# Gate products by tile, three experts set apart, a wider pace of side work, and TensorE given products from the start

## The chip, the cores and the metric

The kernel runs on one core of one Trainium2 chip. The metric is the device time of one execution in microseconds (us). The program works on five engines: TensorE (PE in the rows: matmuls and transposes into PSUM), VectorE (DVE), ScalarE (ACT), GpSimd (POOL) and SyncE (SP, which issues most DMAs). Each engine takes its instructions in the order in which the program wrote them, and waits for the others by semaphores.

## The reference

Three stages in float32. `x` is (4, 8, 512, 64), `state` is (4, 8, 32, 64).

```python
# 1. attention between x and a small state, both ways
a  = softmax(x @ state.T / 8);  xread = a @ state
a2 = softmax(state @ x.T / 8);  sread = a2 @ x
x1 = concat([xread, sread], axis=2)            # -> 2176 rows of 512
# 2. eight experts, every row through all of them, weighted by a Sinkhorn-balanced gate
P = exp(x1 @ w_gate - max)                     # (2176, 8)
for _ in range(8):
    P /= P.sum(1) + 1e-9;  P /= P.sum(0) + 1e-9;  P *= N / E
out = sum_e P[:, e] * (relu(x1 @ w1[e]) @ w2[e])
# 3. the same sizes again, but each row goes to its argmax expert alone
```

w1 is (8, 512, 1024) and w2 is (8, 1024, 512) in both expert stages.

## The kernel before

The 2176 rows are 17 tiles of 128 (`t`). Stage 2 runs in three passes over the rows: tiles 0 to 5, 6 to 11 and 12 to 16. A pass has 32 steps `s`: eight experts, and for each the hidden width in four quarters of 256. A step consists of two parts. `mm1(s)` makes the hidden quarter: seven products of halves of the operands (a scheme that needs seven where the plain one needs eight), each in three float32r matmuls for two halves of the contraction, since every operand is split into a high part and a low part (`XR` holds both for x, `HB` for the hidden values). `mm2(s, t)` multiplies the hidden quarter by w2 for one row tile and adds it to `acc`, weighted by `PG[:, t, e]`, the balanced gate. TensorE runs `mm1(s + 1)` before `mm2(s)`.

Ahead of pass 0 stands the attention for batches 0 and 1 (groups named `A0`, `A1`, `C0`, `C1` in the code, five pieces each: transposes of x (`psx`), scores (`pss`), softmax on VectorE and ScalarE, transposes (`psa`), the read (`pso`)). From its result `xst`, `xsums` and `xsplit` make the seven x operands of pass 0: four sums or differences, seven rounded copies on ScalarE (L390) and seven low parts (L392), of which three go to GpSimd.

All the rest of stage 1 and the gate is side work: it stands in a list named `queue`, and is handed out between the parts of the steps of pass 0. `pump(dt)` adds a nominal time `dt` to a credit (1.04 us for a product of `mm1`, 1.36 us for a tile of `mm2`) and takes one item from the list whenever the credit reaches `pace`. So a small `pace` puts the items close together. The list of before is: the gate products of tiles 0 to 3, 4 to 5 and 6 to 7, the attention of batches 2 and 3 (`window`), the state reads, the gate of tile 16, `close_reads` (which gives back the attention's memory and takes the buffer `raw2` there), and the Sinkhorn steps. The pace is 66 divided by the number of items until `close_reads`, and 2.4 after it.

The Sinkhorn loop is eight times `row` (five small VectorE operations, the last of which, L332, makes column sums) and `col` (a TensorE product `pscol` with a matrix of ones at L337, and four small VectorE operations). Pass 0 must have `PG` when it weights its first expert. Before, the experts 0 and 1 of pass 0 are summed without weight, expert 0 in `acc` and expert 1 in the memory of `xst`, and are weighted at expert 2 (L541, L542), that is in `mm2(8)`; the list is emptied before step 9.

The lines that the steps of the prediction touch: L137 (ScalarE issues the loads of the state), L390 and L392 (operands of pass 0), L376 to L379 (their sums), L432 (GpSimd, low part of the weight sums of the next step), L303 (gate products), L328 to L341 (Sinkhorn), L536 to L547 (what `mm2` does with its PSUM bank).

Of the kernel before, what the change touches and what calls it, by code (L numbers as in the profile page):

```python
# [21 lines left out]
def tile_state_attention_moe_moe2(  # L22
# [104 lines left out]

    def constants():
        make_identity(nc, ident)
        nc.vector.memset(ones, 1.0)  # L130

# [13 lines left out]
    def routing_constants():  # L145
        fl = dict(allow_small_or_imprecise_dtypes=True)
        nc.gpsimd.memset(onesb, 1.0)
        nc.gpsimd.memset(lowb, 1.0)
# [162 lines left out]
    def sinkhorn():  # L311
# [31 lines left out]

        steps += [s0, s1]
        for i in range(8):
            steps += [row, col(i)]
        return steps
# [33 lines left out]

    def xsplit(p, t, order=(0, 4, 3, 5, 1, 2, 6), pool=(3, 1, 6)):
        b11, b12, b21, b22, w = xquarters(p)
        of = [b11, b21, b22] + t

        def one(i):
            def f():
                hi = xop(i, 0, w).rearrange("p (k n) -> p k n", k=2)
                lo = xop(i, 1, w).rearrange("p (k n) -> p k n", k=2)
                nc.scalar.copy(hi, of[i])  # L390
                e = nc.gpsimd if i in pool else nc.vector
                e.tensor_tensor(out=lo, in0=of[i], in1=hi.bitcast(F32), op=ALU.subtract)  # L392
            return f
        return [one(i) for i in order]
# [58 lines left out]
    def mm1(s, between):  # L453
# [39 lines left out]
        between(3)  # L493
        prod(2, B_[1], start=False)
        tt(out=c22, in0=B_[5], in1=u3, op=ALU.add)
        relu(B_[1], 0, 0)
        relu(c22, 1, 1)
        between(4)
        new(3)
        rest(B_[1], 0, 0)  # L500
        tt(out=u4, in0=B_[3], in1=u4, op=ALU.add)  # L501
# [371 lines left out]
    with tc.manual_schedule():  # L873
        accf = acc.rearrange("p a c -> p (a c)")
        crit, lag = {}, {}
        for b in range(B):
            for g in range(G):
                crit[b, g], lag[b, g] = attention(b, g)
        load_x(0, 0)
        constants()  # L880
        load_state(0)
# [26 lines left out]
        A0[4]()  # L908
        A1[4]()
        C0[3]()  # L910
        C1[2]()
        C1[3]()
        C0[4]()
        C1[4]()
        sums, T0 = xsums(0, accf)
        parts = xsplit(0, T0)
        parts[0]()
# [29 lines left out]
        def window(b):  # L947
# [4 lines left out]
            def nx(g, f):  # L952
                def h():
# [7 lines left out]
                    c[1], n20, e[1], c[2], n21, e[2], c[3], nx(0, n30), e[3],  # L961
                    nx(1, n31), c[4], e[4], gate(range(4 * b, 4 * b + 4))]

        home = [None]

        def close_reads():
# [5 lines left out]
            smp[0] = rtp[0]  # L972
            pace[0] = 2.4
            raw2 = ctx.enter_context(tc.tile_pool(name="raw2", bufs=1, side="right", reuse_waits="tile")).tile(
# [52 lines left out]
        queue += window(2) + window(3)  # L1027
        (a0, a1, a2), (b0, b1, b2) = lag[2, 0], lag[2, 1]
        queue += [a0, b0, a1, b1, seq(a2, lambda: load_x(3, 0)), seq(b2, lambda: load_x(3, 1))]
        (a0, a1, a2), (b0, b1, b2) = lag[3, 0], lag[3, 1]  # L1030
        queue += [a0, b0, a1, b1, a2, b2, seq(gate(range(NT - 1, NT)), states_out)]
# [186 lines left out]
```

## Time and profile before

| | |
|---|---|
| median of 3 runs | 1878.95 us (1878.01 to 1881.89) |
| the profiled execution, its own time | 1879.49 us |
| its span in the trace | 1877.8 us |
| TensorE busy | 1804.5 us, 96% of the span |
| VectorE, ScalarE, GpSimd busy | 65%, 35%, 59% |
| granted TensorE clock, mean | 0.973 of full speed |
| the chain that ended last | TensorE 74%, VectorE 9%, issue 9%, DMA 5% |

TensorE is busy nearly all the time, so time can only be lost where it is idle or where it runs at half clock. In the page's forty slices its row falls below 9 tenths at the beginning, in the slices after 200 us, at the two changes of pass (about 660 and 1200 us) and in the last fifth; the granted clock is lowest in the first two slices. A matmul's busy time at half clock counts as busy, and the two must be read together.

### The profile page before, as it was taken

The numbers are of one execution on the slowest core, as the hardware profiler recorded it, in microseconds if no ns is written. First come the engines' busy times: TensorE is split into PE (matmuls) and PEld (weight loads), VectorE is DVE, ScalarE is ACT, GpSimd is POOL, SyncE is SP. The second block draws the span as 40 slices with busy tenths as digits, with TensorE's granted clock in tenths as the row PEclk, the third lists the DMA queues.
The fourth block names the chain that finished last, engine by engine and source line by source line (L and its number), as shares of the span: only waits on it lengthen the run. The fifth ranks groups of instructions, "written<-read, shape, count | busy, mean of one in ns | idle before, by whom it ended". The sixth has DMA issues, their size and how long they took to land.

```text
span 1877.8 us, 25502 instructions
## 1 busy us (share of the span) xinstructions
PE 1804.5 (96%) x9327; PEld 1607.7 (86%) x9327; DVE 1211.8 (65%) x2041; ACT 653.3 (35%) x1114; POOL 1099.3 (59%) x857
## 2 busy tenths in 40 slices
PE   7998899999999999999999999799999999899998
PEld 5997788999999889999999998689999899778886
DVE  5664769666666676666666666896666666745332
ACT  3432222333333333333333333333333343345333
POOL 2432456666776566666667765577787877412212
PEclk8799899999999999999999999899999999999999
DMA  4243112322222222222222222232222222245122
GB/s 113 74 107 96 51 45 68 102 68 68 68 68 68 90 80 71 70 71 96 68 68 68 68 67 84 67 129 81 80 79 79 90 79 68 76 137 199 62 81 89
DMA packets 126618, 154.65 MB, mean 82 GB/s; under 512 B 41424, under 2 KB 91600, under 8 KB 123920
## 3 DMA queue, kind: packets, MB, share of 16 engines
q1 hardware_dynamic: 121920, 142.41, 24.2%
q0 software_dynamic: 3280, 10.23, 1.7%
q8 instruction: 75, 1.23, 0.3%
q14 instruction: 63, 0.52, 0.1%
q10 hardware_dynamic: 1280, 0.26, 0.1%
HBM read 138.99 MB, written 14.42 MB: 82 GB/s over the span
## 4 chain that ended last, share of the span: by engine, by line
PE 74%; DVE 9%; issue 9%; DMA 5%; POOL 2%; ACT 1%; SPq 0%; POOLq 0%; DVEq 0%; ACTq 0%
PE py L527 12%; PE py L528 12%; PE py L529 12%; PE p L465 11%; PE p L467 11%; PE p L466 11%; DMA out_dram<-xst,si 4%; DMA out_dram<-y,si 1%; DVE HB L478 1%; PE psg L303 1%; PE psr L281 1%; PE pss L206 1%; PE pl L576 1%; DVE acc L547 1%; PE pso L243 1%
## 5 line engine op out<-in xcount | busy, mean ns | idle before, releaser
L443 POOL TENSOR_TENSOR wl<-rawb,wh 128x1024 fp32r<-128x1024 f32 x96 | 230.8, 2405 | 473.1 <-ACT wh L442 473.1
L465 PE MATMUL p<-XR 128*128 128x384 f32 (+1 forms) x1344 | 447.9, 333 | 4.2 <-ACT XR L390 2.8
L467 PE MATMUL p<-XR 128*128 128x384 f32 (+1 forms) x1344 | 444.1, 330 | 4.1 <-POOL XR L432 3.0
L466 PE MATMUL p<-XR 128*128 128x384 f32 (+1 forms) x1344 | 443.7, 330 | 0.9 <-DVE XR L392 0.9
L527 PE MATMUL py<-wh,HB 128*128 128x512 f32 x1088 | 431.6, 397 | 2.4 <-DVE acc L547 2.3
L528 PE MATMUL py<-wl,HB 128*128 128x512 f32 x1088 | 429.0, 394 | 0.0
L529 PE MATMUL py<-wh,HB 128*128 128x512 f32 x1088 | 428.6, 394 | 0.0
L547 DVE SCALAR_TENSOR_TENSOR acc<-py,PG,acc 128x512 f32<-128x512 f32 x485 | 338.9, 741 | 79.3 <-PE py L529 78.7
L432 POOL TENSOR_TENSOR XR<-sst,XR 128x1024 fp32r<-128x1024 f32 x96 | 255.0, 2656 | 50.8 <-ACT XR L426 50.8
L465 PEld LDWEIGHTS p<-XR 128*128 128x128 f32 x1344 | 256.8, 191 | 11.3 <-ACT XR L390 4.1
L467 PEld LDWEIGHTS p<-XR 128*128 128x128 f32 x1344 | 256.5, 191 | 5.4 <-POOL XR L432 3.8
L466 PEld LDWEIGHTS p<-XR 128*128 128x128 f32 x1344 | 256.7, 191 | 4.9 <-DVE XR L392 1.5
L478 DVE SCALAR_TENSOR_TENSOR HB<-u,HB 128x384 fp32r<-128x384 f32 (+1 forms) x192 | 169.3, 883 | 117.4 <-ACT HB L474 117.2
L529 PEld LDWEIGHTS py<-wh,HB 128*128 128x128 f32 x1088 | 206.7, 190 | 44.2
L527 PEld LDWEIGHTS py<-wh,HB 128*128 128x128 f32 x1088 | 206.8, 190 | 44.0 <-DVE acc L547 3.0
L528 PEld LDWEIGHTS py<-wl,HB 128*128 128x128 f32 x1088 | 206.6, 190 | 39.7
L483 ACT COPY u<-p 128x384 f32<-128x384 f32 (+1 forms) x96 | 44.3, 461 | 527.6 <-PE p L467 523.5
L428 POOL TENSOR_TENSOR XR<-rawb,XR 128x512 fp32r<-128x512 f32 x96 | 141.6, 1475 | 7.4 <-ACT XR L422 7.4
L426 ACT CAST XR<-sst 128x1024 fp32r<-128x1024 f32 x96 | 100.8, 1050 | 93.7 <-POOL sst L421 93.7
L474 ACT ACTIVATE HB<-u 128x384 fp32r<-128x384 f32 (+1 forms) x192 | 96.9, 505 | 80.0 <-DVE u L501 72.2
L486 DVE TENSOR_TENSOR u<-p,u 128x384 f32<-128x384 f32 (+1 forms) x96 | 51.3, 534 | 112.6 <-PE p L467 108.2
L474 ACT ACTIVATE HB<-p 128x384 fp32r<-128x384 f32 (+1 forms) x96 | 45.5, 474 | 190.4 <-PE p L467 190.4
(292 smaller groups left out, 2491.4 us busy)
## 6 DMA issues: line engine op xcount, KB each, us to landing
rawb<-in_moe_w_dram SPq DMA_DIRECT2D x192, 512.0 KB, 3.5
raw<-in_moe_w_dram SPq DMA_DIRECT2D x15, 1024.0 KB, 6.4
xb<-in_x_dram SPq DMA_DIRECT2D x60, 128.0 KB, 3.1
rawb<-in_moe_w_dram SPq DMA_DIRECT2D x5, 1024.0 KB, 5.1
x1d<-acc SPq DMA_DIRECT2D x16, 256.0 KB, 2.4
xtd<-xtm SPq DMA_DIRECT2D x4, 512.0 KB, 3.0
x1p<-acc SPq DMA_DIRECT2D x8, 256.0 KB, 2.6
xst<-xtd SPq DMA_DIRECT2D x1, 1536.0 KB, 8.3
```

The costliest lines, as they stand in the source:

```text
L428: nc.gpsimd.tensor_tensor(out=wop(s, 1, 0, 2).rearrange(r, k=KD), in0=raw[:, :, 0:P], in1=wop(s, 0, 0, 2).rearrange(r, k=KD).bitcast(F32), ...
L432: nc.gpsimd.tensor_tensor(out=wop(s, 1, 3, 4), in0=sst.rearrange("p a c -> p (a c)"), in1=wop(s, 0, 3, 4).bitcast(F32), op=ALU.subtract)
L443: nc.gpsimd.tensor_tensor(out=lo, in0=raw, in1=hi.bitcast(F32), op=ALU.subtract)
L465: nc.tensor.matmul(ps, wh, xh, start=start and k == 0, stop=False, skip_group_check=True)
L466: nc.tensor.matmul(ps, wh, xl, start=False, stop=False, skip_group_check=True)
L467: nc.tensor.matmul(ps, wl, xh, start=False, stop=stop and k == 1, skip_group_check=True)
L474: nc.scalar.activation(out=hh[:, f, half * h : (half + 1) * h], in_=c, func=AF.Relu)
L478: nc.vector.scalar_tensor_tensor(out=hl[:, f, q], in0=c, scalar=0.0, in1=hh[:, f, q].bitcast(F32), op0=ALU.max, op1=ALU.subtract)
L527: nc.tensor.matmul(ps, hh[:, j, r], whi[:, j, :], start=(j == 0), stop=False)
L528: nc.tensor.matmul(ps, hh[:, j, r], wlo[:, j, :], start=False, stop=False)
L529: nc.tensor.matmul(ps, hl[:, j, r], whi[:, j, :], start=False, stop=(j == 1))
L547: nc.vector.scalar_tensor_tensor(out=a, in0=ps, scalar=PG[:, t, e : e + 1], in1=a, op0=ALU.mult, op1=ALU.add)
```

## The change

Seven edits go together:

- The matrices `ones` and `onesb` are set first on VectorE, and `idle_work(n)` writes `n` products of ones, 256 columns each, into a PSUM bank that nobody reads: 24 ahead of the first transpose, and 3, 3, 4 and 4 within the attention.
- The gate products go tile by tile. Each `gate([t])` has 4 matmuls, and they stand singly between other items. Five of them (tiles 6, 7, 0, 1, 2) are taken in step 0.
- The operands of pass 0: all low parts on VectorE, in another order, and four of the seven within step 0; product 2 of step 0 comes right after product 1.
- The experts 0, 1 and 2 of pass 0 are summed apart (the third in `raw2`); the weights are needed from expert 3 on, in `mm2(12)`. The merging of experts 1 and 2 is 12 items of the list, and `routing_constants` follows them.
- The pace until `close_reads` is 132 divided by the number of items, with a credit that begins at -7.3; 5.6 for the Sinkhorn steps, and 3.6 for the merging.
- A Sinkhorn item is now `col(i)` with the next `row`, so that the column sums of an item are used in the following one; 10 items in place of 18. They come after step 9's products.
- The load of the next pass's x stands at step 20 of a pass in place of step 14.

```diff
     def constants():
+        nc.vector.memset(ones, 1.0)
+        nc.vector.memset(onesb, 1.0)
         make_identity(nc, ident)
-        nc.vector.memset(ones, 1.0)
+    def idle_work(n):
+        wide = ones.bitcast(BF)
+        ps = bank("idle")
+        for _ in range(n):
+            nc.tensor.matmul(ps[:, 0 : 2 * P], onesb, wide, start=True, stop=True)
...
-        steps += [s0, s1]
-        for i in range(8):
-            steps += [row, col(i)]
+        steps += [s0, both(s1, row)]
+        for i in range(7):
+            steps.append(both(col(i), row))
+        steps.append(col(7))
...
-    def xsplit(p, t, order=(0, 4, 3, 5, 1, 2, 6), pool=(3, 1, 6)):
+    def xsplit(p, t, order=(0, 4, 3, 5, 1, 2, 6)):
+        pool = (3, 1, 6) if p > 0 else ()
...
         between(0)
+        if s == 0:
+            prod(2, B_[1], start=False)
+            relu(B_[1], 0, 0)
+            between(4)
+            rest(B_[1], 0, 0)
...
+    NRAW = 3
+    home = [None]
+    def apart(e, t):
+        return (xst if e == 1 else home[0])[:, t * DM : (t + 1) * DM]
+    def merge(e, t):
+        a = accv(t)
+        return lambda: nc.vector.scalar_tensor_tensor(out=a, in0=apart(e, t), scalar=PG[:, t, e : e + 1], in1=a,
+                                                      op0=ALU.mult, op1=ALU.add)
...
-        if p == 0 and e < 2:
-            if e == 1:
-                a = xst[:, t * DM : (t + 1) * DM]
+        if p == 0 and e < NRAW:
+            if e > 0:
+                a = apart(e, t)
...
-        if p == 0 and u == 2 * NQ:
+        if p == 0 and u == NRAW * NQ:
             nc.vector.tensor_scalar_mul(a, a, PG[:, t, 0:1])
-            nc.vector.scalar_tensor_tensor(out=a, in0=xst[:, t * DM : (t + 1) * DM], scalar=PG[:, t, 1:2], in1=a,
-                                           op0=ALU.mult, op1=ALU.add)
...
+        idle_work(24)
         state_T(0)
...
+        parts[1]()
         sums[0]()
         sums[1]()
-        parts[1]()
         parts[2]()
-        sums[2]()
-        parts[3]()
-        sums[3]()
-        for f in parts[4:]:
-            f()
+        early = {0: [parts[3], sums[2]], 4: [parts[4]], 1: [parts[5], sums[3]], 2: [parts[6]]}
...
-        queue += [gate(range(0, 4)), gate(range(4, 6)), gate(range(6, 8))]
...
+        queue += [gate([t]) for t in (6, 7, 0, 1, 2)] + spread(window(2), [3, 4, 5], 4)
+        queue += spread(window(3), range(8, 12), 3)
...
-        pace[0] = 66.0 / len(queue)
-        queue += [close_reads] + sinkhorn()
+        pace[0] = 132.0 / (len(queue) - 5)
+        credit[0] = -7.3
+        balance = sinkhorn()
...
-            if s == 9:
-                flush()
-                routing_constants()
-            if p < 2 and u == 14:
+            if p < 2 and u == 20:
                 xload(p + 1)
...
+                if s == 2 * NQ + 1:
+                    flush()
+                    queue += balance
+                if s == NRAW * NQ + 1:
+                    flush()
                 if u > 0:
                     step_mm2(s - 1)
+                if s == NRAW * NQ + 1:
+                    queue += [merge(e, t) for e in range(1, NRAW) for t in tiles_of(0)] + [routing_constants]
+                    pace[0] = 3.6
```

What the change does to the order of instructions is shown at three places. The first is TensorE from the program's start, before, where `stp` is the state of batch 0 and `xb` its x:

```order
L166 MATMUL psst_149<-ident,stp_123 128x128 x2
L195 MATMUL psx_155<-ident,xb_113 128x128 x4
L195 MATMUL psx_161<-ident,xb_113 128x128 x4
L195 MATMUL psx_173<-ident,xb_129 128x128 x4
L195 MATMUL psx_179<-ident,xb_129 128x128 x4
L206 MATMUL pss_185<-sbd_152,xT_154 128x64 x8
L206 MATMUL pss_201<-sbd_152,xT_172 128x64 x8
```

The same place now, from the last of the 24 products of ones:

```order
L138 LDWEIGHTS onesb
L138 MATMUL idle<-ones,onesb 128x256
L173 MATMUL psst_175<-ident,stp_124 128x128 x2
L202 MATMUL psx_181<-ident,xb_119 128x128 x4
L202 MATMUL psx_187<-ident,xb_119 128x128 x4
L138 LDWEIGHTS onesb
L138 MATMUL idle<-ones,onesb 128x256
L138 LDWEIGHTS onesb
L138 MATMUL idle<-ones,onesb 128x256
L138 LDWEIGHTS onesb
L138 MATMUL idle<-ones,onesb 128x256
L202 MATMUL psx_203<-ident,xb_130 128x128 x4
```

The products of ones stand ahead of the first transpose and between the groups; the attention's own instructions keep their order here. The second place is ScalarE at the end of the attention and the beginning of step 0, before; `XR<-xst` and `XR<-acc` are the rounded operands of pass 0 and `stp` the state loads of batches 2 and 3:

```order
L390 CAST XR<-xst 128x768
L390 CAST XR<-acc 128x768 x3
L390 CAST XR<-xst 128x768 x2
L390 CAST XR<-acc 128x768
L137 DMA stp_393<-in_state_dram 32x2x64 x4
L137 DMA stp_399<-in_state_dram 32x2x64 x4
L483 COPY u_103<-p_0_412 128x384
L442 CAST wh_428<-rawb 128x1024
```

The same place now:

```order
L406 CAST XR<-xst 128x768
L406 CAST XR<-acc 128x768
L145 DMA stp_427<-in_state_dram 32x2x64 x4
L145 DMA stp_433<-in_state_dram 32x2x64 x4
L499 COPY u_103<-p_0_446 128x384
L406 CAST XR<-acc 128x768
L490 ACTIVATE HB<-p_0_446 128x384
L406 CAST XR<-acc 128x768
L406 CAST XR<-xst 128x768
L458 CAST wh_496<-rawb 128x1024
L406 CAST XR<-acc 128x768
```

Before, the eight DMA issues stood behind all seven operands; now four of the seven operands stand behind the issues. The third place is VectorE in the Sinkhorn loop, before: one `col` and the next `row`, with the copies of `mm2` around them:

```order
L536 COPY xst<-py_0_1687 128x512
L338 TENSOR_SCALAR sm_411<-pscol_1695 128x8
L339 RECIPROCAL sm_411<-sm_411 128x8
L340 TENSOR_SCALAR sm_411<-sm_411 128x8
L341 TENSOR_TENSOR PG<-PG,sm_411 128x136
L536 COPY xst<-py_1_1701 128x512
L536 COPY xst<-py_2_1709 128x512
L328 TENSOR_REDUCE sm_408<-PG 128x17
L329 TENSOR_SCALAR sm_408<-sm_408 128x17
L330 RECIPROCAL sm_409<-sm_408 128x17
L331 TENSOR_TENSOR PG<-PG,sm_409 128x136
L332 TENSOR_REDUCE sm_410<-PG 128x8
```

The same place now:

```order
L574 TENSOR_TENSOR raw_2243<-py_0_2388,raw_2243 128x512
L345 TENSOR_SCALAR sm_445<-pscol_2396 128x8
L346 RECIPROCAL sm_445<-sm_445 128x8
L347 TENSOR_SCALAR sm_445<-sm_445 128x8
L348 TENSOR_TENSOR PG<-PG,sm_445 128x136
L335 TENSOR_REDUCE sm_442<-PG 128x17
L336 TENSOR_SCALAR sm_442<-sm_442 128x17
L337 RECIPROCAL sm_443<-sm_442 128x17
L338 TENSOR_TENSOR PG<-PG,sm_443 128x136
L339 TENSOR_REDUCE sm_444<-PG 128x8
L574 TENSOR_TENSOR raw_2243<-py_1_2407,raw_2243 128x512
L574 TENSOR_TENSOR raw_2243<-py_2_2415,raw_2243 128x512
```

The nine small operations now follow each other, and the next `pscol` on TensorE stands three tiles further on, where before the next `pscol` came one tile after its column sums.

## Rows read from the trace of the kernel before

**Rows 1.** Windows: stretch, its length, each engine's busy time, granted clock, DMA share, GB/s.
```profile
6.00:40.00 34.00, 29.22 (x132) 23.70 (x132) 17.58 (x34) 15.07 (x29) 7.11 (x7) 0.85 0.41 95
40.00:70.00 30.00, 27.26 (x107) 26.00 (x108) 15.76 (x22) 8.67 (x14) 12.58 (x10) 0.54 0.34 93
70.00:110.00 40.00, 38.50 (x251) 34.00 (x250) 27.68 (x53) 16.51 (x34) 19.22 (x16) 1.00 0.44 113
110.00:120.00 10.00, 10.00 (x54) 9.21 (x53) 7.42 (x12) 3.37 (x6) 2.78 (x1) 0.83 0.46 127
120.00:200.00 80.00, 74.88 (x453) 67.16 (x452) 47.27 (x94) 27.75 (x63) 24.96 (x21) 0.96 0.30 81
200.00:260.00 60.00, 48.77 (x203) 40.25 (x203) 49.82 (x112) 12.25 (x21) 24.66 (x20) 0.86 0.15 48
260.00:330.00 70.00, 66.51 (x331) 59.42 (x330) 55.35 (x78) 21.34 (x38) 44.40 (x47) 1.00 0.20 61
330.00:600.00 270.00, 270.00 (x1363) 245.26 (x1362) 180.09 (x281) 90.62 (x159) 191.13 (x146) 1.00 0.24 75
```

**Rows 2.** Timeline of TensorE: start, length, instruction, count, idle before it.
```profile
6.03 0.66 PE L166 MATMUL psst<-ident,stp 128*128 128x128 f32 x2 [6.03 <-DMA stp<-in_state_dram]
18.29 1.91 PE L195 MATMUL psx<-ident,acc 128*128 128x128 f32 x8
...
70.20 1.04 PE L195 MATMUL psx<-ident,xb 128*128 128x128 f32 x8
```

**Rows 3.** The chain that ended last, in order of time: start, length, what.
```profile
26.73 1.09 PE psa L231 x4
27.82 3.31 PE pss L206 x16
...
39.76 0.74 ACT XR L390
40.52 0.96 DVE XR L392
41.48 0.88 DVE acc L376
...
54.42 0.32 PE p L466
...
106.30 3.47 PE psg L303 x32
```

**Rows 4.** Timeline of the other engines in step 0 and step 1.
```profile
45.07 1.85 POOL L392 TENSOR_TENSOR XR<-acc,XR 128x768 fp32r<-128x768 f32 x1 [11.54 <-ACT XR L390]
45.17 2.57 DVE L378 TENSOR_TENSOR acc<-xst 128x768 f32<-128x768 f32 x1
...
53.29 3.66 ACTq L137 DMA_DIRECT2D stp<-in_state_dram  x8
...
57.00 0.48 ACT L483 COPY u<-p 128x384 f32<-128x384 f32 x1 [4.01 <-DMA stp<-in_state_dram]
...
71.20 2.46 POOL L432 TENSOR_TENSOR XR<-sst,XR 128x1024 fp32r<-128x1024 f32 x1 [5.56 <-ACT XR L426]
```

**Rows 5.** Waits of TensorE, 200 to 340 us.
```profile
PE pscol L337 <- DVE sm L332: 11.2, 6, 3.7
```

**Rows 6.** Timeline of VectorE in the Sinkhorn loop.
```profile
228.65 2.30 DVE L340 TENSOR_SCALAR sm<-sm 128x8 f32<-128x8 f32 x1
...
235.97 0.17 DVE L340 TENSOR_SCALAR sm<-sm 128x8 f32<-128x8 f32 x1
```

**Rows 7.** The same stretch on GpSimd.
```profile
228.54 2.39 POOL L432 TENSOR_TENSOR XR<-sst,XR 128x1024 fp32r<-128x1024 f32 x1 [2.40 <-ACT XR L426]
```

**Rows 8.** VectorE's groups by line, 190 to 320 us: count, busy us, mean ns, idle before.
```profile
L541 DVE TENSOR_SCALAR acc<-acc,PG 128x512 f32<-128x512 f32 x6 | 6.8, 1126 | 0.0
L542 DVE SCALAR_TENSOR_TENSOR acc<-xst,PG,acc 128x512 f32<-128x512 f32 x6 | 5.6, 930 | 0.2
L340 DVE TENSOR_SCALAR sm<-sm 128x8 f32<-128x8 f32 x8 | 5.4, 670 | 0.3
```

More of the change, by code (lines that the diff above doesn't have):

```diff
@@ L146, in routing_constants @@
         fl = dict(allow_small_or_imprecise_dtypes=True)
-        nc.gpsimd.memset(onesb, 1.0)
         nc.gpsimd.memset(lowb, 1.0)
@@ L342, in col, with both, h @@
             return f
-        steps += [s0, s1]
-        for i in range(8):
-            steps += [row, col(i)]
+        def both(f, g):
+            def h():
+                f()
+                g()
+            return h
+        steps += [s0, both(s1, row)]
+        for i in range(7):
+            steps.append(both(col(i), row))
+        steps.append(col(7))
         return steps
@@ L493, in mm1 @@
         between(3)
-        prod(2, B_[1], start=False)
+        if s > 0:
+            prod(2, B_[1], start=False)
         tt(out=c22, in0=B_[5], in1=u3, op=ALU.add)
-        relu(B_[1], 0, 0)
+        if s > 0:
+            relu(B_[1], 0, 0)
         relu(c22, 1, 1)
-        between(4)
+        if s > 0:
+            between(4)
         new(3)
-        rest(B_[1], 0, 0)
+        if s > 0:
+            rest(B_[1], 0, 0)
         tt(out=u4, in0=B_[3], in1=u4, op=ALU.add)
@@ L878, in tile_state_attention_moe_moe2 @@
                 crit[b, g], lag[b, g] = attention(b, g)
+        constants()
         load_x(0, 0)
-        constants()
         load_state(0)
@@ L890, in tile_state_attention_moe_moe2 @@
         A0[0]()
+        idle_work(3)
         load_x(1, 1)
@@ L893, in tile_state_attention_moe_moe2 @@
         A0[1]()
+        idle_work(3)
         A1[1]()
@@ L902, in tile_state_attention_moe_moe2 @@
         C0[1]()
+        idle_work(4)
         A0[3]()
@@ L909, in tile_state_attention_moe_moe2 @@
         A1[4]()
+        idle_work(4)
+        C1[2]()
         C0[3]()
-        C1[2]()
+        sums, T0 = xsums(0, accf)
+        parts = xsplit(0, T0, (0, 1, 4, 3, 5, 2, 6))
+        parts[0]()
         C1[3]()
@@ L961, in window @@
                     c[1], n20, e[1], c[2], n21, e[2], c[3], nx(0, n30), e[3],
-                    nx(1, n31), c[4], e[4], gate(range(4 * b, 4 * b + 4))]
-        home = [None]
+                    nx(1, n31), c[4], e[4]]
         def close_reads():
@@ L972, in close_reads @@
             smp[0] = rtp[0]
-            pace[0] = 2.4
+            pace[0] = 5.6
             raw2 = ctx.enter_context(tc.tile_pool(name="raw2", bufs=1, side="right", reuse_waits="tile")).tile(
@@ L1002, in between @@
             def between(i):
+                if s == 0:
+                    for f in early.get(i, ()):
+                        f()
+                    if i in (0, 4, 1, 2, 3):
+                        queue.pop(0)()
                 if i == 1:
@@ L1026, in tile_state_attention_moe_moe2, with spread @@
         load_state(3)
-        queue += window(2) + window(3)
-        (a0, a1, a2), (b0, b1, b2) = lag[2, 0], lag[2, 1]
-        queue += [a0, b0, a1, b1, seq(a2, lambda: load_x(3, 0)), seq(b2, lambda: load_x(3, 1))]
-        (a0, a1, a2), (b0, b1, b2) = lag[3, 0], lag[3, 1]
-        queue += [a0, b0, a1, b1, a2, b2, seq(gate(range(NT - 1, NT)), states_out)]
-        pace[0] = 66.0 / len(queue)
-        queue += [close_reads] + sinkhorn()
+        def spread(fs, ts, n):
+            fs, out_ = list(fs), []
+            for t in ts:
+                out_ += fs[:n] + [gate([t])]
+                del fs[:n]
+            return out_ + fs
+        queue += [gate([t]) for t in (6, 7, 0, 1, 2)] + spread(window(2), [3, 4, 5], 4)
+        queue += spread(window(3), range(8, 12), 3)
+        (a0, a1, a2), (b0, b1, b2) = lag[2, 0], lag[2, 1]
+        (c0, c1, c2), (d0, d1, d2) = lag[3, 0], lag[3, 1]
+        queue += spread([a0, b0, a1, b1, seq(a2, lambda: load_x(3, 0)), seq(b2, lambda: load_x(3, 1)), c0, d0, c1, d1, c2, d2],
+                        range(12, 16), 2)
+        queue += [seq(gate([NT - 1]), states_out), close_reads]
+        pace[0] = 132.0 / (len(queue) - 5)
+        credit[0] = -7.3
+        balance = sinkhorn()
         for s in range(3 * NU):
             p, u = divmod(s, NU)
-            if s == 9:
-                flush()
-                routing_constants()
-            if p < 2 and u == 14:
+            if p < 2 and u == 20:
                 xload(p + 1)
```

3 lines of the change are left out of this document (removed).

## The prediction

> **What bounds the kernel now.** I read the windows first, then TensorE's timeline, then the chain that ended last, then the waits. In the windows, see that from 330 us on TensorE is busy 270 of 270 us at full clock: there only fewer or cheaper matmuls could help, and the change makes none fewer. What can be gained lies before 330 us [rows 1], as idle time and as work at half clock. The granted clock has two levels, 1.2 and 2.4 GHz, so a mean of 0.86 means that 28% of the stretch was at the lower one, and half of the work done there is lost.
>
> In the first stretch the clock column misleads: it shows 0.85 for 6 to 40 us, yet eight transposes take 1.91 us at 18 us and 1.04 us at 70 us [rows 2], so TensorE ran at half speed, though it was busy 29 of 34 us. Between 40 and 70 us the mean is 0.54: step 0 ran almost wholly at 1.2 GHz. Half clock comes back at 110 us, right behind 32 gate matmuls of 8 columns that took 3.47 us [rows 3], and in the Sinkhorn stretch, 200 to 260 us, which has 11.2 us of idle time and a mean of 0.86 [rows 1]; `pscol` alone waited 11.2 us there for VectorE's column sums [rows 5].
>
> **The change part by part.** The sum is made against the profiled execution's own time, 1879.49 us, which is 0.5 us above the median.
>
> *The start, up to the weights of step 1.* TensorE waits until 6.03 us for the state [rows 2]. A matmul of 384 columns takes 0.32 us at half clock [rows 3], so 256 columns take about 0.21 us, and 24 products about 5.1 us from some 1.2 us on: they end at about 6.3 us, hidden but for 0.3 us. The other 14 cost 1.5 to 3 us, in places where TensorE waits for the softmax. If they bring the clock up, I count half of those TensorE pieces that lie on the chain behind the last x block: eight transposes 1.91, psa 1.09, pss 3.31 us [rows 2, 3]; half of 6.3 is 3.1. The rest of the attention is VectorE and ScalarE and stays. So its end moves from 39.8 us, where the chain passes to the operands [rows 3], to about 36.7 us. At worst nothing moves and the 0.3 us is lost.
>
> Step 0 is then not TensorE's. I add up its operands by the order of now: copy 0.74, low part 0.96, two sums of 0.88, copy 0.74, low part 0.96 [rows 3], a memset 0.3. Now ScalarE stands at eight DMA issues, which took 3.66 us before, and the copy behind them waited 4.01 us [rows 4]. Before, this fell where TensorE was busy with gates; now four of seven operands are late behind it. After it come the product's copy 0.48 [rows 4], then copy 0.74 and low part 0.96; a sum and such a pair, 2.6; two operations on the products, 1.1, and a low part 0.96; a sum, an operation and a low part, 2.4; small gate copies 0.5. With the 5.5 us ahead and the 3.7 us of issues, the last operand is there 18.9 us after the attention. Four more operations on products (2.2), a copy (1.05) and GpSimd's L432 (2.46, [rows 4]) make the weights of step 1 ready after 24.7 us, at 61.4 us. Before, L432 ended at 73.66 us [rows 4]. Gain 12.2 us. By then TensorE still owes three gates (each a quarter of 3.47 us: 2.6 together), the eight transposes (1.04), four more (0.4) and the state's (0.4): 4.5 us. Waiting behind the issues it falls to half clock, I think, and comes back only some time after it is fully fed: 2 us. The net gain is 5.7 us. Bounds: 0, if the attention stays cold and owed work runs at half clock; 15, if the issues hide.
>
> The low parts taken from GpSimd are no loss: beside GpSimd's 1.85 us the sum L378 took 2.57 us on VectorE [rows 4], against 0.88 for one alone [rows 3], and GpSimd comes earlier to step 1's weights.
>
> *Attention of batches 2 and 3, 74 to 200 us.* Now lost: idle 1.5, 0 and 5.1 us in the three windows; at half clock 17% of 10 us twice, so 1.7 lost, and 8% of 80 us, so up to 3.2 lost [rows 1]. Together 11.5 us. Items come every 2.24 nominal us (132 over 59 items) in place of 1.27 (66 over 52), and a gate is 0.87 us between long products, so neither chains nor a row of gates should stop TensorE; I leave 2.3 us. Gain 9.2 us; bounds 3 and 11.5.
>
> *Sinkhorn and merging, 200 to 330 us.* Now lost: idle 11.2 and 3.5; at half clock 28% of 60 us, of which TensorE was busy 81%, half of that 6.8 [rows 1]: together 21.5 us. Now ten items spread over some 56 us. A `pscol` uses sums made an item earlier, 5.6 us before, so its own wait goes. What is late next is VectorE as a whole. Its regular work is 180 us in 270 [rows 1], 10.3 us per step of 15.4 us (7 products of nominally 1.04 and 6 tiles of 1.36 us). Sinkhorn's nine operations take about 2.5 us undisturbed (for one of them see the 0.17 us in [rows 6]); 2.75 items in a step are 7 us: 17.3 us of VectorE in a step of TensorE's 16. The merging at 3.6 us a piece (0.93 us each, [rows 8]) leaves room. The six scalings L541 (1.13 us each) remain. I leave 6.5 us: some 4 for the backlog, 1 for the scalings, 1.5 for anything else, the first write of the third expert into memory just given back included. Gain 15 us; bounds 2 and 20.
>
> A short operation on SBUF stretches when GpSimd holds one: L340 took 2.30 us from 228.65 us [rows 6], and ends with GpSimd's 2.39 us from 228.54 us [rows 7]. The Trainium skill, "SBUF — State Buffer", section "SBUF: two separate sides", says that VectorE and GpSimd share a port pair that is locked for a whole instruction, also against VectorE operations with two SBUF inputs. The trace agrees (both end at 230.9 us). By that rule each of the 12 merges can wait up to a whole GpSimd operation; it speaks against the merges, and its extreme is the slower rival below.
>
> *Elsewhere.* The load of the next x at step 20 in place of 14 has four steps, some 60 us, until it is used; it costs nothing, and would cost its lateness only if SyncE stood still. Six merges more on VectorE are 5.6 us in three steps with 5 us to spare each. Nothing after 330 us changes.
>
> Sum: 5.7 + 9.2 + 15.0 = 29.9; 1879.5 less 29.9 is 1849.6, and 1849 against the median.
>
> **The rivals.**
>
> *Better: the start is clean.* ScalarE's issues hide or the clock holds through step 0 (+9 us), the backlog is 1 us (+3), the middle clean (+2): gain 44, 1835 us. For it: TensorE has little work in step 0. Against: the 4.01 us wait is in the trace already, and the issues now stand ahead of more.
>
> *Weaker: the clock falls back.* TensorE was busy 29 of 34 us in the attention and stayed at 1.2 GHz [rows 1, 2], so the products of ones may give nothing between them: start 0, and VectorE's backlog twice as long with half clock behind it (c. 8 us less): gain 9.2 + 7 = 16, 1863 us.
>
> *It doesn't do what it says: Sinkhorn stays bound.* VectorE is so full that `pscol` waits as now; the last stretch gains 0 to 2, the others 14.9: 1863 us as well.
>
> *Slower: VectorE is held by GpSimd.* If every Sinkhorn operation on SBUF alone (8 times L331, L340, L341) takes 2.4 us, and the 12 merges and six scalings 2.6 us, VectorE needs in steps 9 to 16 8 x 10.3 + 58 + 31 + 16 + 13 (the small rest) = 200 us where TensorE needs 128. 72 lost, less the 21.5 lost now and the 14.9 gained ahead, is 36 slower: 1915 us. It decides from a loss of 36 us on, that is from a mean of about 1.7 us for these 42 operations. Against: now they take 0.67 to 1.13 us in the mean [rows 8].
>
> **How the numbers follow.** Chances: forecast 0.60, better 0.16, weaker 0.12, Sinkhorn bound 0.06, slower or no change in one way or another 0.06. The forecast's own range is 1840 to 1858; taking in half of the better and most of the weaker case gives 1833 to 1866. 0.2%, 3.8 us, is about what a measurement of this kernel tells from no change. Faster by more has 0.92, within it 0.02, slower 0.06.
>
> **What would show it.** Right: eight transposes near 1 us after the 24 products; the copy of product 1 in step 0 waiting some 4 us behind the state's DMA issues, and TensorE idle there; no wait of `pscol` above 1 us; no window of half clock between 80 and 200 us; step 13 reached some 30 us earlier than now. Wrong: transposes at 1.9 us; step 0 fed without a gap (the gain is larger); VectorE above 95% with TensorE idle between steps 9 and 13 (smaller); any new wait after 330 us.

## The result, and the profile after

The changed kernel takes 1861.68 us (median of 4 runs, 1858.39 to 1861.94) where the kernel before takes 1880.42 us on the same chip (1878.01 to 1882.7): a ratio of 0.9896 [0.9878, 0.9915], 18.7 us faster. 1849 was forecast, in a range of 1833 to 1866. The profiled execution took 1861.75 us, its span is 1860.0 us against 1877.8, and TensorE is busy 1792.6 us of it, still 96%.

The lines of the changed kernel have other numbers: the product's first copy is L499 (L483 before), the state's loads L145 (L137), the gate products L310 (L303), GpSimd's low part of the weight sums L448 (L432) and its low part of w2 L459 (L443), `pscol` L344 (L337), the column sums L339 (L332), `rest` L494 (L478), the scalings L577 (L541), the merges L552 (L542).

The windows of the changed kernel, with the columns of [rows 1]:

```profile
6.00:40.00 34.00, 24.50 (x149) 18.44 (x147) 20.00 (x33) 14.90 (x27) 7.11 (x7) 0.85 0.40 95
40.00:70.00 30.00, 21.29 (x85) 21.20 (x86) 16.86 (x28) 9.94 (x16) 9.36 (x8) 0.55 0.35 93
70.00:110.00 40.00, 39.22 (x232) 35.83 (x231) 30.27 (x56) 16.31 (x31) 22.72 (x17) 0.99 0.29 79
110.00:120.00 10.00, 10.00 (x67) 9.72 (x66) 5.95 (x12) 4.02 (x9) 5.43 (x6) 1.00 0.19 52
120.00:200.00 80.00, 80.00 (x459) 69.33 (x458) 57.86 (x96) 26.13 (x52) 33.85 (x27) 1.00 0.38 106
200.00:260.00 60.00, 60.00 (x363) 55.34 (x362) 38.42 (x75) 22.42 (x47) 29.02 (x24) 1.00 0.29 84
260.00:330.00 70.00, 61.06 (x297) 54.88 (x296) 61.11 (x130) 19.02 (x34) 36.81 (x31) 0.93 0.18 61
```

Count a window's loss as its idle time plus (1 - clock) of the busy time, as the prediction did. Then 70 to 200 us lost 11.3 us before and 1.2 now, a gain of 10.1 (9.2 forecast): from 110 us on TensorE is busy all the time, at full clock. 200 to 330 us lost 21.6 us before and 13.2 now, all of it behind 260 us: a gain of 8.4 (15.0 forecast). The spans differ by 17.8 us, so the start gave 17.8 - 10.1 - 8.4 = -0.7 us where 5.7 were forecast. (At the first copy of step 16 the lead is 19.0 us; without what is lost behind it the start gave 0.5.) Either way it gave nothing, and the window of step 0 by itself says the same: 40 to 70 us lost 15.3 us before and 18.3 now.

TensorE in the changed kernel, where [rows 2] stood for before:

```profile
1.28 4.88 PE L138 MATMUL idle<-ones,onesb 128*128 128x256 bf16 x24 [1.28 <-DVE onesb L130]
...
6.52 1.04 PE L202 MATMUL psx<-ident,xb 128*128 128x128 f32 x8
...
18.98 0.85 PE L202 MATMUL psx<-ident,xb 128*128 128x128 f32 x4 [2.48 <-DMA xb<-in_x_dram]
...
20.90 3.52 PE L213 MATMUL pss<-sbd,acc 128*128 128x64 f32 x16
```

The first transposes are at full clock, 1.04 us for eight. But TensorE then waits 2.48 us for an x block, and the scores behind it take 3.52 us, half clock as in [rows 3]. The attention ends at 40.7 us, where 36.7 was forecast and 39.8 stood before. This end differs from execution to execution: in the eleven traces of this document that have the products of ones ahead of it, it lies between 38.1 and 41.6 us, and never at 36.7. So two or three us between two traces at this place say little by themselves.

Step 0 in the changed kernel, all engines:

```profile
46.48 3.71 ACTq L145 DMA_DIRECT2D stp<-in_state_dram  x8
...
50.23 0.48 ACT L499 COPY u<-p 128x384 f32<-128x384 f32 x1 [5.05 <-DMA stp<-in_state_dram]
...
50.77 0.69 PE L481 MATMUL p<-XR 128*128 128x384 f32 x1 [8.71 <-ACT u L499]
```

```profile
52.85 1.71 PE L310 MATMUL psg<-wg,xtm 128*128 128x8 f32 x8
```

(The second fence is TensorE alone.) Product 2 adds into the bank of product 1, so it must wait until ScalarE has copied that bank, and the copy stands behind an operand of ScalarE's and eight DMA issues: TensorE idles for 8.71 us, and step 0 then runs at half clock until 70.2 us, busy without a gap (a gate product 1.71 us, [rows 3] has a quarter of 3.47 for one at full clock).

The waits of TensorE from 200 to 340 us, as [rows 5]:

```profile
PE pscol L344 <- DVE sm L339: 8.9, 4, 4.5
```

VectorE and GpSimd ahead of the third and the last of these four waits, as [rows 6, 7]:

```profile
302.33 1.96 DVE L336 TENSOR_SCALAR sm<-sm 128x17 f32<-128x17 f32 x1
...
313.78 2.43 DVE L494 SCALAR_TENSOR_TENSOR HB<-u,HB 128x384 fp32r<-128x384 f32 x1 [0.61 <-ACT HB L490]
...
319.21 0.18 DVE L336 TENSOR_SCALAR sm<-sm 128x17 f32<-128x17 f32 x1
...
319.72 2.03 DVE L338 TENSOR_TENSOR PG<-PG,sm 128x136 f32<-128x136 f32 x1
```

```profile
301.85 2.40 POOL L459 TENSOR_TENSOR wl<-rawb,wh 128x1024 fp32r<-128x1024 f32 x1 [7.20 <-ACT wh L458]
...
313.39 2.39 POOL L448 TENSOR_TENSOR XR<-sst,XR 128x1024 fp32r<-128x1024 f32 x1 [4.33 <-ACT XR L442]
...
319.22 2.37 POOL L459 TENSOR_TENSOR wl<-rawb,wh 128x1024 fp32r<-128x1024 f32 x1 [3.44 <-ACT wh L458]
```

The same L336 takes 1.96 us beside a GpSimd operation and 0.18 us alone; 302.33 + 1.96 and 301.85 + 2.40 are the same moment, and so are 319.72 + 2.03 and 319.22 + 2.37 within 0.2 us. `rest` (L494) takes 2.43 us from 313.78, while L448 runs until 315.78, and 0.55 us just before it.

### The profile page after: what moved, and what is told of

The parts are those of the page before. It is cut to its first block, busy times and chain, and to the rows that moved or that the text cites. A ratio compares the mean times of both kernels' runs of the same rounds, so it can differ in the third digit from the quotient of the medians.

```text
span 1860.0 us, 25570 instructions
## 1 busy us (share of the span) xinstructions
PE 1792.6 (96%) x9365; PEld 1599.0 (86%) x9365; DVE 1223.7 (66%) x2062; ACT 653.0 (35%) x1114; POOL 1093.6 (59%) x853
## 4 chain that ended last, share of the span: by engine, by line
PE 74%; issue 12%; DVE 7%; DMA 4%; POOL 2%; ACT 1%; SPq 1%; POOLq 0%; DVEq 0%; ACTq 0%
PE py L563 12%; PE py L564 12%; PE py L565 12%; PE p L481 11%; PE p L483 11%; PE p L482 11%; DMA out_dram<-xst,si 2%; DMA out_dram<-y,si 1%; DVE HB L494 1%; PE psr L288 1%; PE pl L610 1%; DVE acc L581 1%; POOL XR L448 1%; PE psg L310 1%; PE pf L599 0%
## 5 line engine op out<-in xcount | busy, mean ns | idle before, releaser
L459 POOL TENSOR_TENSOR wl<-rawb,wh 128x1024 fp32r<-128x1024 f32 x96 | 232.4, 2421 | 473.2 <-ACT wh L458 473.2
L483 PE MATMUL p<-XR 128*128 128x384 f32 (+1 forms) x1344 | 444.9, 331 | 4.1 <-POOL XR L448 2.9
L581 DVE SCALAR_TENSOR_TENSOR acc<-py,PG,acc 128x512 f32<-128x512 f32 x461 | 321.6, 740 | 73.1 <-PE py L565 72.5
L448 POOL TENSOR_TENSOR XR<-sst,XR 128x1024 fp32r<-128x1024 f32 x96 | 252.8, 2634 | 53.8 <-ACT XR L442 46.4
L483 PEld LDWEIGHTS p<-XR 128*128 128x128 f32 x1344 | 256.9, 191 | 5.6 <-POOL XR L448 4.1
L494 DVE SCALAR_TENSOR_TENSOR HB<-u,HB 128x384 fp32r<-128x384 f32 (+1 forms) x192 | 181.9, 949 | 114.8 <-ACT HB L490 114.6
L499 ACT COPY u<-p 128x384 f32<-128x384 f32 (+1 forms) x96 | 44.3, 461 | 497.9 <-PE p L483 492.9
```

Source lines behind the costliest of these rows:

```text
L448: nc.gpsimd.tensor_tensor(out=wop(s, 1, 3, 4), in0=sst.rearrange("p a c -> p (a c)"), in1=wop(s, 0, 3, 4).bitcast(F32), op=ALU.subtract)
L459: nc.gpsimd.tensor_tensor(out=lo, in0=raw, in1=hi.bitcast(F32), op=ALU.subtract)
L483: nc.tensor.matmul(ps, wl, xh, start=False, stop=stop and k == 1, skip_group_check=True)
L494: nc.vector.scalar_tensor_tensor(out=hl[:, f, q], in0=c, scalar=0.0, in1=hh[:, f, q].bitcast(F32), op0=ALU.max, op1=ALU.subtract)
L581: nc.vector.scalar_tensor_tensor(out=a, in0=ps, scalar=PG[:, t, e : e + 1], in1=a, op0=ALU.mult, op1=ALU.add)
```

## The experiments

All are the changed kernel with one edit, unless another is named. Given are the median time, and the ratio to the kernel before on the same chip with its 95% interval; the ratio of the changed kernel is 0.9896.

### The state by SyncE

```diff
-            nc.scalar.dma_start(out=stp[...], in_=sv[q])
+            (nc.scalar if b < 2 else nc.sync).dma_start(out=stp[...], in_=sv[q])
```

> The changed kernel, with the eight state loads of batches 2 and 3 issued by SyncE in place of ScalarE; nothing is left out. Theory: step 0 is held because product 2 adds to the bank of product 1, must wait until ScalarE has copied that bank, and this copy stands behind 3.7 us of DMA issues. Then TensorE's 8.7 us wait falls below 2 us, product 2 begins near 42 us in place of 50.8, the copy of step 1's first product comes at 57 to 63 us in place of 71.1, and the time is 1846 to 1854 us where the changed kernel had 1861.7. Rival: VectorE's chain of operands or the half clock sets the end of step 0 anyway; then step 1's copy stays within 3 us of 71 and the time within 3 us of 1861.7.

1856.49 us, 0.9862 [0.9847, 0.9878]. TensorE in step 0:

```profile
45.64 0.69 PE L481 MATMUL p<-XR 128*128 128x384 f32 x1 [3.56 <-ACT u L499]
...
47.72 1.71 PE L310 MATMUL psg<-wg,xtm 128*128 128x8 f32 x8
```

The wait shrinks to 3.56 us, where less than 2 was expected: what is left is the operand ahead of the copy, for which ScalarE waits 2.94 us for VectorE's sums. All later steps come 4.6 to 5.4 us earlier (the copy of step 8 at 216.47 in place of 221.62), and the time is 5.2 us shorter, 2.5 us short of the range expected. So the issues were the larger part of the wait. But 3.56 us of idling are followed by half clock as well: step 0 stays there until 65.9 us.

### Without products of ones

The five calls of `idle_work` are taken out.

> The changed kernel without the 38 products of ones. Theory: the full clock that they bring is lost again at about 18 us, while TensorE waits for the last x block, so the end of the attention (40.7 us) and of step 0 (70.2 us) stay within 1.5 us and the time within 3 us of 1861.7. Rival: the warm start shortens the attention, and without it everything is 4 to 8 us later, 1866 to 1870 us.

1860.91 us, 0.9896 [0.9881, 0.9911]: the time of the changed kernel. The first transposes take 1.91 us again, yet step 0's copy comes at 47.8 us, no later than with the products (50.2). TensorE:

```profile
10.90 0.63 PE L202 MATMUL psx<-ident,xb 128*128 128x128 f32 x4 [1.22 <-DMA xb<-in_x_dram]
...
19.92 3.37 PE L213 MATMUL pss<-sbd,acc 128*128 128x64 f32 x16
```

So TensorE reaches full clock without the products, too (four transposes in 0.63 us at 10.9 us), and in both kernels it is at half clock again behind the waits for x at 18 to 20 us (scores in 3.37 and 3.52 us). What the products bring up at 1 to 6 us serves a few us of work and doesn't last.

### Products of ones in the wait of step 0

The kernel with the state by SyncE, and:

```diff
         if s == 0:
+            idle_work(32)
             prod(2, B_[1], start=False)
```

> The kernel with the first state by SyncE, and 32 products of ones more in step 0, ahead of product 2, where TensorE waited 3.6 us for ScalarE's copy. Theory A, this wait is what puts step 0 at half clock: with it filled, product 2 and the gates run at full clock (a gate 0.95 us, as at 41 us, in place of 1.71), step 1's first copy comes at 59 to 61 us in place of 66.2, and the time is 4 to 6 us below that of the kernel with the state by SyncE (1856.5), about 1851.5. Rival B, the gates (matmuls of 8 columns) bring the clock down by themselves: the gates after the first one or two are again at 1.71 us, the copy comes at 64 to 66 us, and the time is within 2 us of 1856.5. Rival C, the operands decide: full clock, but TensorE idles for the low parts, the copy comes at 62 to 64 us, 2 to 4 us gained.

1854.23 us, 0.9851 [0.9833, 0.9868]. TensorE in step 0:

```profile
42.84 3.65 PE L138 MATMUL idle<-ones,onesb 128*128 128x256 bf16 x32
...
47.73 0.95 PE L310 MATMUL psg<-wg,xtm 128*128 128x8 f32 x8
...
53.56 0.95 PE L310 MATMUL psg<-wg,xst 128*128 128x8 f32 x8
...
57.53 0.45 PE L481 MATMUL p<-XR 128*128 128x384 f32 x1 [1.13 <-ACT XR L406]
58.76 0.69 PE L482 MATMUL p<-XR 128*128 128x384 f32 x1 [0.78 <-DVE XR L408]
59.25 0.52 PE L483 MATMUL p<-XR 128*128 128x384 f32 x1
```

The wait was the cause of half clock here: with it filled, all five gate products take 0.95 us, so they don't bring the clock down (rival B falls). Then the operands are late (rival C): two waits of 1.13 and 0.78 us, and the clock falls behind them. The copy of step 1 comes at 62.7 us, 3.5 us earlier than with the state by SyncE alone; only 1.0 us of it is left at step 8 (215.45 against 216.47), since step 1 now begins at half clock (0.60 from 60 to 70 us, where the other kernel has 0.71) and waits 1.0 us for GpSimd's L448. 2.3 us were gained where theory A had 4 to 6 and rival C 2 to 4; the two intervals overlap widely, so that the gain in time isn't clear of noise, while the clock in the rows is.

### The gates in blocks

`spread` puts a window's gates behind one another at its end, not singly between the other items.

> The changed kernel with the gate products of tiles 3 to 5, 8 to 11 and 12 to 15 in three blocks again, at the place of the last of each; the five of step 0 and the paces stay. Theory of the prediction: a block of gates brings the clock to its lower level, as after 106 us in the kernel before; then two or three stretches of half clock of 3 to 7 us appear between 110 and 260 us, and the time is 4 to 9 us longer, 1865 to 1871 us. Rival: what freed the stretch from 74 to 260 us was the wider pace alone; then no half clock appears there and the time stays within 2 us of 1861.7.

1867.48 us, 0.9917 [0.99, 0.9935], 5.8 us slower. Its windows:

```profile
110.00:200.00 90.00, 90.00 (x514) 81.78 (x513) 62.52 (x102) 29.79 (x60) 39.52 (x32) 0.94 0.33 90
200.00:260.00 60.00, 58.91 (x335) 52.14 (x334) 33.53 (x63) 19.96 (x44) 24.46 (x21) 0.94 0.30 82
```

Half clock is back in both, 5.4 and 4.6 us of loss with the idle 1.1, where the changed kernel has none, and at the copy of step 16 this trace is 8.5 us behind it. This, 4 to 6 us by the ratios and the times, is what the gate by tile is worth; the intervals just overlap. The 5.1 us that TensorE idled from 120 to 200 us before don't come back with the blocks (90 of 90 us busy): they belong to the wider pace and the rest of the change, which no run takes apart.

### Sinkhorn queued at once

Its items follow the gate's in the list (pace 7.2 in place of 5.6, 116.5 in place of 132 over the items ahead), not from step 9 on.

> The changed kernel with the attention's side work closer (116.5 in place of 132) and the Sinkhorn items one step earlier and wider apart (7.2 in place of 5.6). Theory: VectorE was filled in steps 9 to 13 (9.1 to 9.5 of 10 us busy), so pscol's waits (8.9 us) and the half clock behind them fall below 4 us together, and the time is 5 to 9 us shorter, 1853 to 1857 us. Rival: the waits come from single operations that GpSimd holds up for 2 us, wherever they stand; then the waits stay at 7 to 10 us and the time within 3 us of 1861.7.

1854.94 us, 0.9858 [0.9842, 0.9875]. The waits of `pscol` fall to 6.0 us (three, the longest 3.6), not below 4: less work per step helps, and single operations are still held (L336 2.30 us). The time is as expected.

### Four Sinkhorn rounds

```diff
-        for i in range(7):
+        for i in range(3):
...
-            pace[0] = 5.6
+            pace[0] = 9.3
```

> The changed kernel with four Sinkhorn rounds in place of eight (the other four are left out), one item per 9.3 nominal us in place of 5.6, so that they take as long as the eight did. Theory A, VectorE as a whole is late between 260 and 340 us: about half of Sinkhorn's work goes, the waits of pscol fall from 8.9 to below 2 us, the stretch from 260 to 330 us stays at full clock, and the time falls by 8 to 13 us, to about 1850. Theory B, single operations held by GpSimd decide, whatever VectorE's load: half of the items meet such operations half as often, the waits fall to 4 or 5 us and the time by 3 to 6 us, to about 1857.

The run leaves out half of the rounds. 1850.8 us, 0.9837 [0.9821, 0.9853]. `pscol` waits for nothing, and the stretch is full:

```profile
260.00:330.00 70.00, 70.00 (x363) 64.17 (x362) 60.98 (x109) 23.89 (x42) 44.80 (x36) 1.00 0.20 62
```

That is theory A, at its number. It doesn't say what makes VectorE late, since half of the rounds also meet half as many of GpSimd's operations.

### GpSimd's operations in halves, in quarters

```diff
-            nc.gpsimd.tensor_tensor(out=wop(s, 1, 3, 4), in0=sst..., in1=wop(s, 0, 3, 4)..., op=ALU.subtract)
+            for i in range(0, 4, 2):
+                nc.gpsimd.tensor_tensor(out=wop(s, 1, 3 + i, 2), in0=sst...[:, i * FQ : i * FQ + 2 * FQ],
+                                        in1=wop(s, 0, 3 + i, 2)..., op=ALU.subtract)
...
-        nc.gpsimd.tensor_tensor(out=lo, in0=raw, in1=hi..., op=ALU.subtract)
+        for i in range(0, 1024, 512):
+            nc.gpsimd.tensor_tensor(out=lo[:, i : i + 512], in0=raw[:, i : i + 512], in1=hi[:, i : i + 512]..., op=ALU.subtract)
```

> The changed kernel, its two longest GpSimd operations (the low parts of the weights, 128x1024, 2.4 us each) issued as two of 128x512 each, in all steps. Theory A, VectorE's operations on SBUF stand until GpSimd's one is over, and this is what makes pscol late: none is held longer than some 1.3 us, the last product's low part (L494) falls from 2.43 to about 1.3 us, the waits of pscol fall from 8.9 to below 5 us, and the time by 3 to 6 us, to about 1857. Theory B, it is the sum of VectorE's work that is late: held times shrink one by one, but the second half holds the next operation, pscol still waits 8 us or more, and the time stays within 2 us of 1861.7.

> The changed kernel with GpSimd's two longest operations (128x1024) issued as four of 128x256 each, where the kernel with halves ran at 1845.4 us. Theory A, what counts is how long one GpSimd operation holds a VectorE operation: the last product's low part (L494 of 128x384, 1.51 us in the mean with whole operations, 0.97 with halves) falls to 0.75 or less, the waits of pscol from 5.5 to 3 us or less, and the time by another 2 to 4 us, to about 1842. Theory B, the next short operation just meets the next piece: the held time is the same in sum, GpSimd needs 0.5 us more per operation for its pieces, and the time is within 2 us of 1845.4 or above it.

Halves: 1845.37 us, 0.9806 [0.9793, 0.982]. Quarters: 1839.68 us, 0.9773 [0.9756, 0.979]. VectorE's groups from 240 to 345 us (count, busy us, mean ns, idle before), of the changed kernel, of halves and of quarters:

```profile
L494 DVE SCALAR_TENSOR_TENSOR HB<-u,HB 128x384 fp32r<-128x384 f32 x10 | 15.1, 1511 | 2.2 <-ACT HB L490 2.2
L574 DVE TENSOR_TENSOR raw<-py,raw 128x512 f32<-128x512 f32 x18 | 11.3, 678 | 0.0
L338 DVE TENSOR_TENSOR PG<-PG,sm 128x136 f32<-128x136 f32 x8 | 4.7, 583 | 0.3
...
L336 DVE TENSOR_SCALAR sm<-sm 128x17 f32<-128x17 f32 x8 | 4.4, 545 | 0.3
...
L494 DVE SCALAR_TENSOR_TENSOR HB<-p,HB 128x384 fp32r<-128x384 f32 x5 | 2.8, 551 | 2.7 <-ACT HB L490 2.7
```

```profile
L576 DVE TENSOR_TENSOR raw<-py,raw 128x512 f32<-128x512 f32 x18 | 11.3, 678 | 0.0
L496 DVE SCALAR_TENSOR_TENSOR HB<-u,HB 128x384 fp32r<-128x384 f32 x10 | 9.7, 968 | 2.2 <-ACT HB L492 2.0
```

```profile
L576 DVE TENSOR_TENSOR raw<-py,raw 128x512 f32<-128x512 f32 x18 | 11.3, 679 | 0.0
L496 DVE SCALAR_TENSOR_TENSOR HB<-u,HB 128x384 fp32r<-128x384 f32 x12 | 9.1, 768 | 2.2 <-ACT HB L492 2.0
```

Theory A holds in the main. `rest` of the last two products has both inputs in SBUF, and its mean falls from 1.51 to 0.97 and 0.77 us as GpSimd's pieces get shorter; the same operation with one input in PSUM (`HB<-p`) takes 0.55 us beside whole operations, and the sums out of PSUM (`raw<-py`) 0.68 us in all three. Not every operation gains: `rest` of `c` (`HB<-c`), also with both inputs in SBUF, goes from 0.62 to 0.77 and 0.79 us, and L347 from 0.25 to 0.32 and 0.36, which is theory B's part. `pscol` waits 5.5 us and 3.3 us in place of 8.9, a little more than the 5 and 3 expected. From step 8 to step 16 the lead over the changed kernel grows by 5.4 and 9.0 us, about what theory A gave halves (3 to 6); the total was far more, 16.3 and 22.0 us, for the lead grows by another 7.6 and 13.2 us up to step 72, at the two changes of pass, where no theory had looked. There, too, TensorE waits for VectorE; two of the largest waits, in the changed kernel and then with quarters:

```profile
PE pf L599 <- DVE acc L581: 4.0, 1, 4.0
...
PE pgat L715 <- DVE osg L773: 4.6, 1, 4.6
...
PE pf L601 <- DVE acc L583: 1.6, 1, 1.6
...
PE pgat L717 <- DVE osg L775: 2.9, 1, 2.9
```

From step 30 to 36 TensorE idles 8.1 us in the changed kernel, 6.4 with halves and 5.3 with quarters; from step 62 to 72 it idles 14.1, 11.0 and 9.7 us. Its waits for GpSimd's own low parts there are 3.1, 1.9 and 3.2 us, so weights that are ready piece by piece are at most 1.2 us of the gain. Some 3 us more are the changed kernel's own trace: from step 62 to 72 TensorE is busy 155.9 us in it, 152.6 in the kernel before and 152.8 with four rounds, both with whole operations, and 152.9 with halves. GpSimd pays for the pieces: a piece of 256 columns takes 0.81 to 0.86 us, so four need 3.2 to 3.4 in place of 2.4.

### The kernel before, with halves

> The kernel before, with only GpSimd's two longest operations in halves. Theory A, GpSimd's hold on VectorE cost the kernel before as much as the changed one: 6 us in the Sinkhorn stretch and 5 to 8 us at the passes' ends and later, so 1868 to 1872, 10 to 14 us below before's 1882.3, and the 2.30 us of L340 are not seen again (none above 1.5). Rival: the hold was made worse by the change (more VectorE work close together), and before gains 4 us or less in the Sinkhorn stretch: 1873 to 1877.

1869.4 us, 0.9929 [0.9912, 0.9946]: the time forecast by theory A, but not its places. The Sinkhorn loop's L340 falls from 0.67 to 0.35 us in the mean, yet `pscol` waits as long as in [rows 5]:

```profile
PE pscol L337 <- DVE sm L332: 11.4, 6, 3.0
```

By step 16 it leads the kernel before by 2.4 us; up to step 72 by 11.6, the other 9 at the changes of pass. So before, `pscol` did not wait because of the hold's length; the prediction's reason, that it followed its own sums too closely, fits. The hold took its place only with the change.

### Both moves, all four, all four with quarters

The state by SyncE and Sinkhorn queued at once; the same with the 32 products of ones and halves; and with quarters.

> The kernel with the first state by SyncE and with Sinkhorn queued at once behind the gates (its pace 7.2, that of the attention 116.5 over the items) in one. Alone they gained 6.4 and 7 us at 1861.7 and 1882. If the two gains lie in stretches of their own (before 75 us, after 220 us), they add up: 13 us, about 1848.5. If what the start gives is taken back by VectorE's backlog in the Sinkhorn stretch (earlier start, same VectorE work ahead of step 14), no more than 7 to 9 us: 1853 to 1855.

> The changed kernel with the four edits that helped: first state by SyncE, 32 products of ones ahead of step 0's product 2, Sinkhorn queued at once, GpSimd's two longest operations in halves. By the runs so far (start 6.2 by the markers of step 8, Sinkhorn queued at once 4.1, halves 6.4 in the Sinkhorn stretch and 7.6 behind 580 us), if all add up: 1861.7 - 6.2 - 4.1 - 14 = 1837.5. Rival: the Sinkhorn stretch has no more than 13.2 us to give, of which halves and queue take some together; 8 in place of 10.5: 1840 to 1842.

> The kernel with all four edits, its GpSimd operations in quarters in place of halves. On the changed kernel quarters gained 5.7 us over halves (1839.7 against 1845.4), of which 5.8 us in the Sinkhorn stretch (markers of step 16) and 5.6 us at the passes' ends, less about 2.2 us of a later start in the profile of halves. With Sinkhorn queued earlier the stretch has less to give: 2 to 4 us there and 3 to 5 at the passes' ends, 1828 to 1831. Rival: GpSimd's longer work in pieces (17% more) makes the weights late with less slack, and the time is 1834 to 1838, no better than halves.

1850.12 us, 0.9835 [0.9821, 0.9848]; 1835.82 us, 0.9746 [0.9729, 0.9763]; 1828.0 us, 0.9719 [0.9705, 0.9733]. By the medians of the single runs, full addition would be 1849.8, 1831.2 and 1825.5 us: the gains add up in the first, and all but 2 to 5 us in the others. The last is 33.7 us faster than the changed kernel, and 260 to 330 us is full in it:

```profile
40.00:70.00 30.00, 25.27 (x154) 23.39 (x154) 20.38 (x35) 12.77 (x21) 19.43 (x23) 0.88 0.40 108
...
260.00:330.00 70.00, 69.95 (x356) 62.68 (x354) 66.26 (x133) 21.38 (x37) 50.43 (x63) 1.00 0.21 68
```

## Why the prediction was right in part

The direction and the range held: the gain comes where it was put, ahead of 330 us, and steady steps are as long as before (15.5 us). 11 of the 30 us forecast are missing, and they are missing in two terms. By its parts the result is not the forecast, whose own range ended at 1858, but the rival called weaker, which had a chance of 0.12: start 0, 9.2 and 7, 1863 us. Measured are -0.7, 10.1 and 8.4, 1861.7 us, and its reason for the start, products that give nothing because the clock falls back, is what the rows show.

**The start: 5.7 forecast, -0.7 measured.** Two steps failed. The one that moved the attention's end to about 36.7 us took the clock that the products bring up as kept; it was lost behind a wait for x, and taking the products out changes nothing. And "Step 0 is then not TensorE's" took the operands for the limit. It saw ScalarE's eight issues and TensorE idle and at half clock behind them, but priced the clock at 2 us, a term that stands on no row. In the new order TensorE's very next product waits for the copy behind the issues. The sum has TensorE owe 4.5 us behind the last operand; it owed nearly all of step 0, at half clock, from 50.8 to 70.2 us, and half of these 19.4 us is 9.7 where 2 were put. The lower bound of 0 had named half clock, as owed work. GpSimd's L448 ended at 72.1 us, not 61.4:

```profile
69.72 2.38 POOL L448 TENSOR_TENSOR XR<-sst,XR 128x1024 fp32r<-128x1024 f32 x1 [4.51 <-ACT XR L442]
```

With both causes removed the start does give: the run with the products in the wait leads the changed kernel by 6.2 us at step 8, 5.1 of it by the issues. Traces with the changed kernel's own start lead it by up to 3.2 us there (quarters), so the sizes are rough.

**74 to 200 us: 9.2 forecast, 10.1 measured**, for the reasons given; the run with gates in blocks shows one of them, the half clock behind a row of gates, and leaves the wider pace argued.

**Sinkhorn and merging: 15.0 forecast, 8.4 measured.** The mechanism was right, `pscol`'s own wait went and VectorE as a whole is late next; the remainder was mis-sized, 6.5 us left where 13.2 are: 8.9 us of waits, and 4.3 us of half clock, in the windows of the waits and right behind them. The mis-sized term is the backlog of 4 us. It took VectorE's 10.3 us per step from steps of before, and 2.5 us for Sinkhorn's nine operations from undisturbed ones. With more VectorE work side by side, more of it meets GpSimd: in 105 us, ten `rest` operations at 1.51 us are 9.6 us more than at 0.55, which one takes undisturbed, and L336 (0.55 for 0.18) and L338 (0.58 for 0.30) another 5 us. Part of that was in the sum without being seen: in the steps of before from which the 10.3 us were taken (330 to 600 us) the same `rest` took 0.87 us in the mean, so that 6.4 of the 9.6 us are new. The slower rival had this mechanism, at 36 us and with the Sinkhorn operations, merges and scalings as its victims; these 42 took 0.63 us in the mean, far from the 1.7 that it needed. The mechanism is real, and quarters alone take 9.0 us of it away in that stretch. The largest victim, `rest`, was named in neither sum. The scalings, left at 1.13 us each, took 0.48.

The shared ports of VectorE and GpSimd, as the prediction cites them from the Trainium skill ("SBUF — State Buffer", "SBUF: two separate sides"), agree with the rows: operations with two SBUF inputs stand until GpSimd's one is over (L338, `rest`), those with an input in PSUM do not (0.55 and 0.68 us). L336 and L340, which have one input in SBUF, are held as well (1.96 and 2.30 us), which the prediction's account of it doesn't name.

**What would show it.** Seen: transposes at 1.04 us, the copy behind the issues with TensorE idle, no half clock from 80 to 200 us, step 13 at 317.7 us where it was at 344.8, 27 us earlier (some of this is Sinkhorn's work put off: from step 16 on the lead is 19.0). Not seen: `pscol` without a wait above 1 us (it had four, the longest 4.5 us). The sign for a smaller gain was there in one place: from 270 to 280 us VectorE is busy 9.54 of 10 us and TensorE 8.23.

## What to carry to other kernels

Where VectorE's operations stand until GpSimd's one is over, GpSimd's should be short: cutting two GpSimd operations of 2.4 us into quarters was worth 22 us here, more than the whole change. When products are put in another order, ask for each one whose reader must free its bank first, and what stands ahead of that reader in its own queue, DMA issues included. Work that only keeps the clock up did so where it filled the last wait ahead of a busy stretch (a gate 0.95 in place of 1.71 us), and gave nothing ahead of another wait.

## What was not expected of the hardware

- Once at half clock, TensorE stayed there though it was busy without a gap: from 45.6 to 65.9 us with the state by SyncE, from 50.8 to 70.2 us in the changed kernel. Behind the 24 products of ones (4.88 us) it was at full clock. What brought it back at 66 and 70 us is not settled.
- A wait of 3.6 us ahead of step 0, of 2.5 us in the attention, and two of 1.1 and 0.8 us close together were each followed by half clock. Others were not: one of 1.19 us at 37.5 us with the state by SyncE, and one of 0.78 us at 72.2 us in the changed kernel.
- Eight issues of 16 KB each hold ScalarE for 3.71 us, 0.46 us apiece, and all that it has to do behind them.
- At the changes of pass, too, shorter GpSimd operations left TensorE 4.8 (halves) and 7.2 us (quarters) less idle time, in the main waits for VectorE; which of VectorE's operations are held there is not settled.
